# Six row scatters of a batch, one to each group of score units, with GpSimd in the order of the program text

## The chip, the cores and the metric

The kernel runs on one core of a Trainium2 chip. The metric is the device time of one execution in microseconds (us). A core has five engines that run their own instruction streams: TensorE (PE, matmuls and transposes; its weight loads are shown apart as PEld), VectorE (DVE), ScalarE (ACT), GpSimd (POOL) and SyncE (SP, which here only issues DMAs). They wait for each other through semaphores. An engine executes its own instructions in order, so an instruction that waits holds everything behind it on that engine. DMAs are issued by SyncE (loads of q, k, v, and transposes) and by GpSimd (weight loads that cast to bf16, and the indirect row scatters and gathers), and are carried by the same 16 DMA engines.

## The reference

Two stages. The first is attention with chunk selection: for 4 batches of 8 heads, 768 positions and 64 dimensions, keys are grouped into chunks of 32. Each query scores every chunk by an upper bound and keeps the best six; scores outside of them, or ahead of the query, are masked.

```python
ub = np.sum(np.maximum(q[..., None, :] * k_min, q[..., None, :] * k_max), axis=-1)
ub = np.where(causal, ub, -1e9)
top_chunks = np.argsort(ub, axis=-1)[..., -6:]
scores = np.where(sel & (pos[:, None] >= pos[None, :]), scale * q @ k.T, -1e9)
attn = softmax(scores);  attn_out = attn @ v
```

The second takes the 3072 tokens (512 values each: 8 heads of 64) through a layer of eight experts, one per token:

```python
logits = x @ w_gate
expert_idx = np.argmax(logits, axis=1)          # one expert per token
gate_w = softmax(logits)[expert_idx]
out[token] = gate_w * (np.maximum(x @ w1[e], 0) @ w2[e])
```

## The kernel before

**Units of work.** Two heads of a batch form a head pair; there are 16, numbered i = 0 to 15, four to a batch (b = i // 4, hp = i % 4). A pair's scores are cut into seven units: units 0 and 1 for the first half of the queries, 2 to 6 for the second half. `scores` (line 273) makes a unit's scores on PE, takes the exponential on ScalarE into a tile tagged Pa (units 0 and 2) or Pr (the others), and, where a block lies on the diagonal, lets GpSimd zero the future with `affine_select` (line 298). Units 0, 1, 5 and 6 have such blocks, 1 and 6 two each. `attend` (line 301) multiplies a unit by v on PE (line 311) and adds the unit into an accumulator on VectorE (line 323).

**The loop.** Lines 616 to 662 run over i, and for each i over four groups g = 0 to 3, with the units (0, 1), (2, 3), (4, 5) and (6) of `groups`. Into these groups the program text places, ahead of time or behind it, the steps of neighbouring pairs: the transposes and reductions of the next pairs' keys and queries (`prep`), the bound and selection of pair i + 1 (`ub` in g = 0, line 234; `select` in g = 1, lines 242 to 253; `mask` in g = 2, lines 260 to 263), the loads of q, k and v three pairs ahead (`load`), a quarter of an expert's weights per step (`load_w`, line 173), and the steps of the router for earlier pairs. `ud` (g = 1, lines 339 to 347) forms the denominators and the pair's part of the gate logits, `lgp` (g = 3) adds them to the batch's logits `lg` on GpSimd (lines 362 and 365), `x0` (g = 3) and `x1` (g = 0 of the pair after) transpose the attention output back to rows and write them, normalised, as bf16 into `xrow0` and `xrow1` (line 373).

**Routing of a batch.** When a batch's four pairs are done, `route_steps(b)` chooses the expert (`logits`, lines 381 to 408), ranks the tokens within their experts (`rank`, lines 410 to 431, which ends in the row numbers `sli` on VectorE), and `scatter` (lines 433 to 446) writes the 768 rows of 1032 bytes to a DRAM table `xs_dram`, sorted by expert: six indirect DMAs of 128 rows, numbered u = 0 to 5, even u from `xrow0` and odd u from `xrow1`. The three calls for batch b - 1 stand in the second pair of batch b: logits after g = 0, rank in g = 1, scatters after g = 2 and g = 3. So the pairs i = 5, 9 and 13 carry them. The last batch is routed after the loop.

**Buffers.** `xrow` has three buffers for two tiles per batch, so the `xrow1` of a batch lies where the `xrow0` of the batch before lay. Its first write is `x1` of the batch's first pair, in g = 0 of the batch's third pair (i = 6, 10, 14), and it has to wait until scatters 0, 2 and 4 of the batch before have read their rows. The small PSUM tiles (tag `m`) rotate through three buffers.

**The experts.** After the loop, and from g = 1 of the last pair on, tiles of 128 sorted rows are gathered (`gather`, line 533), transposed by a DMA on SyncE (`x_in`, line 545, with a copy `ti` of the token numbers on VectorE, lines 548 and 550), multiplied by w1 (`up`, line 562), transposed again (line 568), multiplied by w2 (`down`, line 578), scaled (line 582) and scattered to the output (line 583). Gathers 0 to 10 need only the rows of the first three batches, the others those of the last batch too.

**What sets the order.** A scheduler orders each engine's instructions by its own estimate of when they are ready. For engines named in `tc.manual_schedule` the order is that of the program text. Before, this is PE alone in the loop, PE and SyncE after it. A few instructions are pinned with `keep_in_program_order` (weight loads among them). GpSimd's other work, the selects, casts (line 219), additions to `lg`, scatters and gathers, is placed by the scheduler.

Of the kernel before, what the change touches and what calls it, by code (L numbers as in the profile page):

```python
# [15 lines left out]
AX = mybir.AxisListType  # L16
PE = mybir.EngineType.PE
SP = mybir.EngineType.SP


@with_exitstack
def kernel(
# [157 lines left out]
    def load(i):  # L180
        b, hp = divmod(i, HP)
        for nm, src in (("k", k), ("q", q), ("v", v)):
            t_ = ld.tile([128, NT, 2, D], FP32, tag=nm, bufs=2 if nm == "v" else 1)
            for hd in range(2):
                nc.sync.dma_start(out=t_[:, :, hd, :],
                                  in_=src[b, 2 * hp + hd].rearrange("(t p) d -> p t d", p=128))
            st[i][nm] = t_
# [407 lines left out]
    route = {b: route_steps(b) for b in range(B)}  # L595
# [5 lines left out]
    def run(d, j, *names):  # L601
        if j in d:
            for n in names:
                d[j][n]()

    with tc.manual_schedule(engines={PE}):
        load(0)
        load(1)
        load(2)
        run(prep, 0, "k0", "k1", "q0", "q0e", "q1", "q1e", "kse", "ub", "select")  # L610
        run(prep, 1, "k0")
        run(prep, 0, "mask")
        scores(0, 0)
        scores(0, 1)
        run(prep, 1, "k1", "q0", "q0e", "q1", "q1e", "kse")
        for i in range(NP):
            b, hp = divmod(i, HP)
            for g in range(4):
                if g == 0:
                    scores(i, 2)  # L620
                    scores(i, 3)
                    run(rout, i - 2, "x1")
                elif g == 1:
                    scores(i, 4)
                    scores(i, 5)
                    run(prep, i + 1, "select")
                    if hp == 1 and b > 0:
                        route[b - 1][1]()
                elif g == 2:
                    scores(i, 6)  # L630
                    run(prep, i + 2, "k0")
                    run(prep, i + 1, "mask")
                else:
                    run(rout, i - 1, "lgp", "x0")
                    if i + 1 < NP:
                        scores(i + 1, 0)
                        scores(i + 1, 1)
                    run(prep, i + 2, "k1", "q0", "q0e", "q1")
                    if i + 3 < NP:
                        load(i + 3)  # L640
                for u in groups[g]:
                    attend(i, u)
                if g == 3:
                    run(prep, i + 2, "q1e", "kse")
                if g == 0:
                    run(prep, i + 1, "ub")
                    if hp == 1 and b > 0:
                        route[b - 1][0]()
                if g == 1:
                    run(rout, i - 1, "ud")  # L650
                if hp == 1 and b > 0 and g == 2:
                    route[b - 1][2]((0, 2, 4))
                if hp == 1 and b > 0 and g == 3:
                    route[b - 1][2]((1, 3, 5))
                for n in range(NW):
                    if wq[n] == 4 * i + g:
                        load_w(n)
                if i == NP - 2 and g == 2:
                    table(True)
                if i == NP - 1 and g == 1:  # L660
                    for j in range(4):
                        gather(j)
                        x_in(j)
        rt = rout[NP - 1]
        r = route[B - 1]
        run(rout, NP - 2, "x1")
        with tc.manual_schedule(engines={SP}):
            up(0)
            rt["ud"]()
            gather(4)  # L670
            up(1)
            x_in(4)
            rt["lgp"]()
            rt["x0"]()
            rt["x1"]()
            r[0]()
            gather(5)
            up(2)
            x_in(5)
            down(0)  # L680
            r[1]()
            gather(6)
            r[2](range(6))
            table(False)

            def tiles(lo, hi):
                for j in range(lo, hi + 2):
                    if lo == 0 and j < 3:
                        continue
                    if lo == 0 and j + 4 < hi:  # L690
                        gather(j + 4)
                    if j < hi:
                        up(j)
                    if lo == 0 and j + 3 < hi:
                        x_in(j + 3)
                    if j - 2 >= lo:
                        down(j - 2)

            tiles(0, JM)
    rest = nc.values_load(more[0:1, 0:1], min_val=NA - JM, max_val=JT - JM,  # L700
                          skip_runtime_bounds_check_because="the table counts at most one part tile per expert")
    with tc.If(rest > 0):
        with tc.manual_schedule(engines={PE, SP}):
            for j in range(JM, JT):
# [41 lines left out]
```

## Time and profile before

| | us |
|---|---|
| median of 9 runs | 382.86 |
| lowest and highest | 381.7 and 386.67 |
| the profiled execution | 382.29 |
| its span in the profile | 380.4 |
| granted PE clock, mean | 0.962 |
| attention, twelve periods: from the bound of pair 3 to that of pair 15 (56.15 to 238.25) | 182.10 |
| from there to the first expert matmul (238.25 to 261.43) | 23.18 |
| from there to the last output scatter of the timeline (261.43 to 369.39) | 107.96 |

Lines of the profile name the engine, the source line (L436), the operation, the tile written and the tiles read, and the times. A row of a timeline begins with the start in us from the span's start and the busy time; in brackets stands the idle time of the engine before it and what ended it. A row of the table of stages gives, for a stretch of time, its length, the busy time and number of instructions of each engine, the granted PE clock as a share of full speed, the share of time that the DMA engines were busy (it can pass 1 a little in short stretches) and the GB/s they moved. In the experts' part one stretch stands out: from 278.0 to 287.6 PE is busy for 5.90 us of 9.60 at a clock of 0.77, and ScalarE waits 7.6 us for something that the profile names only as remote.

### The profile page before, as it was taken

The numbers are of one execution on the slowest core, as the hardware profiler recorded it, in microseconds if no ns is written. First come the engines' busy times: TensorE is split into PE (matmuls) and PEld (weight loads), VectorE is DVE, ScalarE is ACT, GpSimd is POOL, SyncE is SP. The second block draws the span as 40 slices with busy tenths as digits, with TensorE's granted clock in tenths as the row PEclk, the third lists the DMA queues.
The fourth block names the chain that finished last, engine by engine and source line by source line (L and its number), as shares of the span: only waits on it lengthen the run. The fifth ranks groups of instructions, "written<-read, shape, count | busy, mean of one in ns | idle before, by whom it ended". The sixth has DMA issues, their size and how long they took to land.

```text
span 380.4 us, 7332 instructions
## 1 busy us (share of the span) xinstructions
PE 339.7 (89%) x2214; PEld 171.2 (45%) x2224; DVE 229.1 (60%) x781; ACT 236.5 (62%) x397; POOL 182.2 (48%) x298
## 2 busy tenths in 40 slices
PE   2588999999979999998999997988969899999990
PEld 1244465455444554553545544433523344444430
DVE  7547898898997898995988997956710000000000
ACT  1477797797795977965779777552414454545440
POOL 9232442352386343467423438376375556565231
PEclk9859999999999999998999998999987999999997
DMA  9445989999979989869998985334958999998741
GB/s 171 80 93 101 179 155 155 190 167 155 179 163 208 178 160 181 163 138 203 161 188 165 168 153 93 88 72 112 146 146 179 206 233 190 210 219 182 189 122 47
DMA packets 138182, 59.81 MB, mean 157 GB/s; under 512 B 122779, under 2 KB 130973, under 8 KB 138144
## 3 DMA queue, kind: packets, MB, share of 16 engines
q1 hardware_dynamic: 120608, 29.91, 40.9%
q0 software_dynamic: 17536, 29.42, 40.0%
q8 instruction: 20, 0.33, 0.3%
q14 instruction: 18, 0.15, 0.2%
HBM read 56.14 MB, written 10.51 MB: 175 GB/s over the span
## 4 chain that ended last, share of the span: by engine, by line
PE 50%; ACT 12%; issue 12%; DVE 8%; POOL 7%; DMA 5%; another core or an unknown queue 3%; SPq 0%; POOLq 0%; ACTq 0%
PE po L311 13%; PE ps L289 7%; PE ph L562 6%; PE pu L234 5%; PE py L578 5%; PE pt L371 3%; ACT Pr L294 3%; PE pu L339 3%; ACT QSB L263 3%; ACT QSB L262 3%; PE pu L344 3%; POOL out_dram L583 2%; PE pt L242 2%; PE pt L210 2%
## 5 line engine op out<-in xcount | busy, mean ns | idle before, releaser
L323 DVE TENSOR_TENSOR Pa<-Pa,Pr 128x768 f32<-128x768 f32 (+2 forms) x112 | 82.2, 734 | 6.2 <-PE po L311 4.1
L298 POOL TENSOR_SCALAR_AFFINE_SELECT Pr<-Pr 128x256 f32<-128x256 f32 x80 | 33.7, 440 | 72.8 <-ACT Pr L294 71.9
L294 ACT ACTIVATE Pr<-ps 128x768 f32<-128x768 f32 (+2 forms) x112 | 65.3, 628 | 3.5 <-PE ps L289 3.1
L578 PE MATMUL py<-w_all,hT 128*128 x219 | 54.1, 385 | 4.2 <-issue 2.7
L289 PE MATMUL ps<-QSB,KTE 128*128 128x384 bf16 (+2 forms) x288 | 50.0, 297 | 3.6 <-ACT QSB L263 2.5
L583 POOL DMA_INDIRECT out_dram<-y,ti x28 | 27.8, 994 | 42.3 <-ACT y L582 29.9
L289 PEld LDWEIGHTS <-KTE 128*128 128x128 bf16 x288 | 24.5, 99 | 35.0 <-issue 26.7
L578 PEld LDWEIGHTS <-hT 128*128 128x128 bf16 x224 | 22.0, 98 | 32.6 <-issue 5.4
L436 POOL DMA_INDIRECT xs_dram<-xrow,sli x24 | 26.9, 1121 | 13.8 <-issue 5.3
L562 PE MATMUL ph<-w_all,KTE 128*128 x117 | 29.2, 391 | 0.3 <-issue 0.2
L347 ACT ACTIVATE ud<-pu 128x384 f32<-128x384 f32 x16 | 7.9, 492 | 34.2 <-PE pu L344 34.2
L294 ACT ACTIVATE Pa<-ps 128x768 f32<-128x768 f32 x32 | 26.0, 812 | 3.7 <-PE ps L289 3.0
L562 PE MATMUL ph<-w_all,QSB 128*128 x102 | 24.9, 379 | 2.0 <-issue 1.8
L173 POOL DMA_DIRECT2D w_all<-in_moe_w_dram x32 | 24.5, 765 | 0.0
L202 DVE TENSOR_REDUCE kmx<-pt 128x12 f32<-128x384 f32 x32 | 17.7, 554 | 7.8 <-PE pt L200 7.7
L219 POOL CAST QSB<-qT 64x384 bf16<-64x384 f32 x32 | 16.2, 515 | 11.6 <-DVE qT L217 11.2
L582 ACT ACTIVATE y<-py,xg 128x512 f32<-128x512 f32 x16 | 11.0, 688 | 14.4 <-PE py L578 6.3
L245 DVE TENSOR_TENSOR ubm<-pt,cbias 128x144 f32<-128x144 f32 x32 | 8.6, 302 | 18.8 <-PE pt L242 18.6
L373 DVE TENSOR_TENSOR xrow<-pt,rec 128x384 bf16<-128x384 f32 x32 | 17.6, 551 | 2.9 <-DMA xs_dram<-xrow,sli 2.2
L533 POOL DMA_INDIRECT xg<-xs_dram,grow x16 | 17.0, 1061 | 4.8 <-issue 4.4
L550 DVE TENSOR_TENSOR ti<-xg,inv_i 128x1 int32<-128x1 int32 x9 | 1.4, 159 | 29.6 <-DMA xg<-xs_dram,grow 28.4
L562 PEld LDWEIGHTS <-KTE 128*128 128x128 bf16 x120 | 12.0, 100 | 15.8 <-issue 3.3
(294 smaller groups left out, 659.1 us busy)
## 6 DMA issues: line engine op xcount, KB each, us to landing
w_all<-in_moe_w_dram POOLq DMA_DIRECT2D x32, 512.0 KB
out_dram<-y,ti POOLq DMA_INDIRECT x28
t__188<-in_k_dram SPq DMA_DIRECT2D x2, 192.0 KB
t__191<-in_q_dram SPq DMA_DIRECT2D x2, 192.0 KB
t__194<-in_v_dram SPq DMA_DIRECT2D x2, 192.0 KB
t__203<-in_v_dram SPq DMA_DIRECT2D x2, 192.0 KB
t__197<-in_k_dram SPq DMA_DIRECT2D x2, 192.0 KB
t__200<-in_q_dram SPq DMA_DIRECT2D x2, 192.0 KB
```

What stands on the lines that cost most here:

```text
L173: d = nc.gpsimd.dma_start(out=dst, in_=src.rearrange("(c p) f -> p c f", p=128))
L202: nc.vector.tensor_reduce(s["kmx"][:, ts(hf, 12)], pk, AX.X, ALU.max)
L234: nc.tensor.matmul(pu[64 * hf:64 * hf + 64, :], lhsT=w_[:], rhs=s[f"{nm}{hf}"][:], start=(nm == "qT"), stop=(nm == "qA"), skip_group_check ...
L289: nc.tensor.matmul(pv[:, hd, :], lhsT=kte[:, hd, ts(kb, 128)], rhs=qsb[:, hd, ds(qb * 384 + 384 - w, w)], start=True, stop=True, skip_grou ...
L294: nc.scalar.activation(P[:, :, ds(c0, w)], pv, AF.Exp)
L298: nc.gpsimd.affine_select(out=pd, in_=pd, pattern=[[0, 2], [1, 128]], compare_op=ALU.is_ge, fill=0.0, base=0, channel_multiplier=-1)
L311: nc.tensor.matmul(po[64 * hd:64 * hd + 64, 384 - w:384], lhsT=vt[:, kb, hd, :], rhs=P[:, hd, ds(c0, w)], start=first, stop=last and n == ...
L323: nc.vector.tensor_tensor(acc[:, :, 384 - w:384], acc[:, :, 384 - w:384], P[:, :, ds(c0, w)], ALU.add)
L436: d = nc.gpsimd.indirect_dma_start(out=xs_dram[:], out_offset=bass.IndirectOffsetOnAxis(ap=sli[:, u:u + 1], axis=0), in_=bst[b][f"xrow{u % ...
L562: nc.tensor.matmul(ph[:, fh, :], lhsT=xT[:, c, :], rhs=w_all[:, ds(wo + (c * F + fh * 512), 512)], start=(c == 0), stop=(c == NDC - 1), sk ...
L578: nc.tensor.matmul(py[:], lhsT=hT[:, c, :], rhs=w_all[:, ds(wo + (W1W + c * DM), DM)], start=(c == 0), stop=(c == NFC - 1))
L583: d = nc.gpsimd.indirect_dma_start(out=out[:], out_offset=bass.IndirectOffsetOnAxis(ap=fs[j]["ti"], axis=0), in_=y[:], in_offset=None, bou ...
```

## The change

The scatters of a batch are called one at a time, after six groups in a row, from g = 2 of the second pair to g = 3 of the third, in the order u = 0, 2, 4, 1, 3, 5. GpSimd joins PE in the list of engines whose instructions keep the order of the program text within the loop (and, since the block after the loop is nested in it, there too). What is scattered and the number of DMAs stay. Line numbers in the changed kernel are one higher from line 19 to the loop.

```diff
+POOL = mybir.EngineType.Pool
...
-    with tc.manual_schedule(engines={PE}):
+    with tc.manual_schedule(engines={PE, POOL}):
...
-                if hp == 1 and b > 0 and g == 2:
-                    route[b - 1][2]((0, 2, 4))
-                if hp == 1 and b > 0 and g == 3:
-                    route[b - 1][2]((1, 3, 5))
+                slot = 4 * hp + g - 6
+                if b > 0 and 0 <= slot < 6:
+                    route[b - 1][2]((2 * (slot % 3) + slot // 3,))
```

In the order of the built program, the changed kernel has on GpSimd, in a pair that routes: the two selects of unit 6, scatter 0, a weight load, the addition to `lg`, the selects of units 0 and 1 of the next pair, two casts, and then, already for the next pair, scatters 2 and 4 and a weight load, the select of unit 5, scatter 1, the selects of unit 6, scatter 3, a weight load, and behind that pair's casts scatter 5. In the last pair: scatter 5, the select of unit 5, gathers 0 to 3, the selects of unit 6, two additions to `lg`, gather 4, two additions, gather 5, the first output scatter, gather 6, the last batch's six scatters, gather 7. On VectorE line 373 of the third pair moves from ahead of the accumulations to between the two additions of line 245.

## The prediction

> **What bounds the kernel now.** I read the page's first part, then cut the span into the periods of a head pair with the table of stages, because the chain that ended last repeats itself nearly word for word from 56 to 238 us. A period runs from one start of the bound matmul (line 234) to the next.
>
> ```profile
> PE 339.7 (89%) x2214; PEld 171.2 (45%) x2224; DVE 229.1 (60%) x781; ACT 236.5 (62%) x397; POOL 182.2 (48%) x298
> ```
> ```profile
> 84.53:98.73 14.20, 14.12 (x111) 7.57 (x108) 12.53 (x40) 11.64 (x22) 5.32 (x13) 1.00 0.94 171
> 98.73:115.80 17.07, 14.86 (x123) 7.93 (x120) 15.47 (x56) 13.28 (x25) 10.34 (x15) 1.00 0.89 160
> 115.80:129.93 14.13, 14.05 (x110) 7.49 (x108) 12.07 (x39) 10.33 (x19) 8.61 (x17) 1.00 1.08 202
> ...
> 158.30:176.62 18.32, 16.12 (x123) 8.55 (x120) 15.69 (x56) 13.28 (x25) 11.27 (x15) 0.93 0.83 154
> 176.62:191.46 14.84, 14.51 (x111) 7.61 (x110) 12.33 (x38) 10.33 (x19) 7.49 (x16) 0.98 1.07 195
> ...
> 219.88:238.25 18.37, 16.13 (x122) 8.59 (x120) 15.67 (x56) 13.24 (x25) 10.65 (x15) 0.92 0.67 117
> ```
> Columns: stretch, length, then busy time of PE, PEld, DVE, ACT, POOL, clock, DMA share, GB/s. A plain period is 14.2 us and PE is busy for 14.1 of it: PE is the bound, with nothing to gain. The three periods that route a batch (head pairs 5, 9, 13) take 17.07, 18.32 and 18.37 us. Why, the timeline of GpSimd, then of PE and VectorE, shows (first routing period, then the same wait of PE and of VectorE in the others):
>
> ```profile
> 105.64 1.58 POOL L436 DMA_INDIRECT xs_dram<-xrow,sli  x1 [2.29 <-DVE sli L429]
> 107.21 1.46 POOL L298 TENSOR_SCALAR_AFFINE_SELECT Pr<-Pr 128x256 f32<-128x256 f32 x2
> 108.84 1.29 POOL L436 DMA_INDIRECT xs_dram<-xrow,sli  x1 [0.17 <-issue]
> 110.44 0.98 POOL L436 DMA_INDIRECT xs_dram<-xrow,sli  x1 [0.30 <-issue]
> 111.40 0.80 POOL L173 DMA_DIRECT2D w_all<-in_moe_w_dram  x1
> 112.50 1.04 POOL L436 DMA_INDIRECT xs_dram<-xrow,sli  x1 [0.30 <-issue]
> 113.53 0.34 POOL L362 TENSOR_TENSOR lg<-lgt 128x48 f32<-128x48 f32 x1
> 113.77 0.46 POOL L298 TENSOR_SCALAR_AFFINE_SELECT Pa<-Pa 128x256 f32<-128x256 f32 x1
> ```
> ```profile
> 114.28 0.87 PE L311 MATMUL po<-Pa,t__1094 128*64 128x384 f32 x4 [1.82 <-POOL Pa L298]
> ...
> 173.85 1.50 PE L311 MATMUL po<-Pa,t__1951 128*64 128x384 f32 x4 [1.82 <-POOL Pa L298]
> ...
> 235.42 1.55 PE L311 MATMUL po<-Pa,t__2808 128*64 128x384 f32 x4 [1.83 <-POOL Pa L298]
> ```
> ```profile
> 114.10 0.56 DVE L373 TENSOR_TENSOR xrow<-pt,rec 128x384 bf16<-128x384 f32 x1 [0.56 <-DMA xs_dram<-xrow,sli]
> ...
> 174.51 0.56 DVE L373 TENSOR_TENSOR xrow<-pt,rec 128x384 bf16<-128x384 f32 x1 [1.37 <-DMA xs_dram<-xrow,sli]
> ...
> 234.98 0.56 DVE L373 TENSOR_TENSOR xrow<-pt,rec 128x384 bf16<-128x384 f32 x1 [0.28 <-DMA xs_dram<-xrow,sli]
> ```
> The diagonal select of Pa had its input at about 109.5 (ACT 108.68 + 0.81) and ran at 113.77, behind three scatters and a weight load; PE stood 1.82 us for it, three times. The last rows are the price list for what the change touches: line 373 writes the buffer that the scatters 0, 2, 4 read, and goes on only when scatter 4 has landed: 3.66, 4.50 and 3.41 us after that scatter's start (110.44, 170.01, 231.57).
>
> **The change part by part.** Times within a period are counted from U, the start of line 234 (in a plain period 84.53).
>
> *1. No scatter between the selects of a routing period.* The built program's order on GpSimd is now: two selects of unit 6, scatter 0, weight load, lg, Pa, Pr, two casts, scatters 2 and 4. Scatter 0 (1.29) from 106.8, weight load (0.80), lg (0.34): Pa could go at 109.5 and be done at 109.9, while PE asks for it at 112.46 (111.91 + 0.55). Cover 2.5 us, so the three waits go: 1.82 + 1.82 + 1.83 = -5.5.
>
> *2. The slow clock behind them.* After the second and third wait the next matmuls took 1.50 instead of 0.87 and the clock of the period is 0.93 and 0.92; after the first, the same wait cost nothing. By periods: (18.32 + 14.84) - (17.07 + 14.13) = 2.0 for the second; 18.37 - 17.07 = 1.3, and about 0.3 after it, for the third. Gone: -3.5 (ends 0 and -3.6).
>
> *3. Scatter 0 no longer waits for sli in front of the selects.* The selects of unit 6 ran at 107.21, ready at 106.0; VectorE waited 0.15 for them and PE 0.23 at line 210. Some 0.3 each: -0.9 (ends 0 and -1.2). What stays is routing itself: VectorE has 15.47 busy us in such a period against 12.53, so I expect some 15.0 us, not 14.2.
>
> *4. The new wait.* Scatter 4 is now the last but in the next period: behind the second cast (end U - 0.7) and scatter 2 it starts near U + 0.8. Line 373 of the first head pair of the new batch has to wait for it and stands in VectorE's new order between the two additions of line 245. Behind it wait the second addition, the maxima and nsel (line 253), and for nsel PE's mask transposes (line 260), then ACT's copies and the next scores. From plain rows: nsel ends 3.03 us after line 373 starts (0.48, then 87.31 to 89.86), and PE asks at U + 6.09 (90.62). So line 373 may start at U + 3.06 for free. With a landing of 3.66 it starts at U + 4.46: PE stands 1.40. I take 3.66 (the middle row) for the first two batches and 3.41 for the third, where no loads of q, k, v follow: 1.40 + 1.40 + 1.15 = +3.9. The ends: the fastest gather's 2.83 us (249.31 to 252.14) gives 0.57 each, +1.7; 4.50 everywhere gives 2.24 each, +6.7. The transposed tile that line 373 reads is held as long; the next user is line 200 at U + 5.66, not late at 3.66.
>
> [...]
>
> *5. Clock behind the new wait.* Waits of 1.82 cost 0.1, 2.0 and 1.6 in clock; the gaps of 0.52, 0.44 and 1.10 in head pair 15 cost none (0.99 over 238.25 to 261.43). The new ones lie between: I take the mean of the three, once, +1.2 (ends 0 and 3 x 1.8 = 5.4).
>
> [...]
>
> *6. Head pair 15 and the gathers.* Scatter 5 of the third batch now stands before that pair's last selects, and gather 0 waits for it (issued about 250.3, landed by 253.7 at 3.41), then the gathers 0 to 3 (four of 1.31 with their gaps, 5.2 us) come between the select of unit 5 (253.8) and those of unit 6. PE's gaps of 0.52 (POOL) and 0.44 (VectorE, held by ti of line 548) go, the one of 1.10 at unit 6 becomes about 2. Net +0.2 (ends -1.0 and +1.5).
>
> *7. Tail.* Gathers 4 to 7 leave 256.6 to 263 and go behind lg, the first output scatter and the six last scatters: about 262.5, 268.5, 273.3, 282.4. SyncE takes their transposes in its fixed order at 268.99, 272.10, 275.57 and 285.44, so 4 and 5 are in time, 6 about 0.6 late, 7 level; behind a late one waits only the next hT. ScalarE's 7.6 us wait at 275.5 and PE's slow stretch from 278 to 287.6 cover these; if they went, gather 7 would become the next thing late. Later gathers come one tile (3.45) later with some 10 us of lead: 0. The six last scatters start 1.3 later; nothing reads them before gather 11 at 291. Weight loads only move by a few us, needed from 261: 0. DMA counts are the same.
>
> Sum: -5.5 - 3.5 - 0.9 + 3.9 + 1.2 + 0.2 = -4.6. The profiled run took 382.29 (span 380.4 and 1.9 around it), 0.57 under the median of 382.86. 382.29 - 4.6 = 377.7.
>
> **The rivals.**
> - *The wait is hidden* (scatter 4 lands within 2.8 us): for it, the gathers' 2.83 us and that the burst of SP loads ends near U + 1.6; against it, the three scatter rows. -9.9 + 0.2 + 0 to 1.7 = 372.6 to 374.3.
> - *The clock falls at every new wait*: for it, two of three before; against it, the new waits are shorter. -9.9 + 3.9 + 0.2 + 5.4 = -0.4: 381.9, no change.
> - *Slower*: the same place, line 373, with landings of 4.5 and more in each batch, since scatter 4 now follows a weight load and shares the engines with the next loads, and the clock falls as well: 6.7 + 5.4 + 0.2 - 9.9 = +2.4, 384.7. It decides from 3.3 us lost per batch (9.9 / 3); against it, only one row of three was 4.50.
> - *The change does nothing*, because another wait ends last in PE's place: against it, PE is named behind POOL in all three, and in the first VectorE ended KD at 113.53, which line 234 would ask for at 112.46 + 1.44 = 113.90 at the earliest. If VectorE held PE nearly as long, only what part 2 saves without the new wait's cost remains: 380 to 382.
>
> **How the numbers follow.** My forecast 0.54, hidden wait 0.15, clock at every wait 0.12, nothing 0.06, slower 0.13. About 0.5% (1.9 us) is what a measurement of this kernel can tell from no change. Faster by more (under 380.9): forecast, hidden, and a third of nothing: 0.71. Within: clock, rest of nothing: 0.16. Slower: 0.13. The likeliest case's own range is 375 to 380.5; for 8 in 10 the range leaves out half of the hidden wait's times and the slower case: 373.2 to 383.0.
>
> **What would show it.** Right: PE's three waits on Pa gone, routing periods near 15.0; line 373 waiting 1 to 2 us on the scatter in the periods after, PE waiting for nsel there, those periods near 15.6. Wrong: those periods at 14.2 (wait hidden) or above 17 (clock below 0.95); a gap of more than 3 us at unit 6 in pair 15; a longer or shorter stretch at 278 to 288, which nothing in this profile explains and which I hold fixed.

## The result, and the profile after

The changed kernel takes 392.74 us (median of 10 runs, 391.1 to 396.0); the kernel before took 383.78 us on the same chips (31 runs, 379.5 to 389.5). The ratio is 1.027, with a 95% interval from 1.023 to 1.030: slower by 2.7%, where the prediction had 377.7 us and a range up to 383.0. The profiled execution took 391.39 us, with a span of 389.6; that of before took 382.29, with a span of 380.4. Line numbers of the changed kernel are one higher than before: the 373 of the prediction is 374 here.

The first part of the page of the changed kernel shows an unchanged amount of work; PE's share fell by a point:

```profile
PE 342.4 (88%) x2214; PEld 172.3 (44%) x2224; DVE 227.8 (58%) x781; ACT 236.3 (61%) x397; POOL 180.3 (46%) x298
```

The table of stages of the changed kernel, cut at the starts U of line 235 (its first matmul in the timeline, 0.17 us before the point that the prediction counts from; columns as in the prediction: length, then busy time of PE, PEld, DVE, ACT, POOL, clock, DMA share, GB/s):

```profile
85.17:99.36 14.19, 14.11 (x113) 7.56 (x110) 12.52 (x39) 11.64 (x22) 5.30 (x13) 1.00 0.92 169
99.36:114.14 14.78, 14.63 (x124) 7.93 (x122) 14.49 (x55) 11.78 (x23) 6.81 (x14) 1.00 0.93 142
114.14:133.82 19.68, 15.78 (x112) 8.47 (x110) 12.54 (x39) 11.63 (x22) 10.21 (x17) 0.91 0.95 182
...
162.19:176.98 14.79, 14.64 (x125) 7.94 (x122) 14.50 (x55) 11.79 (x23) 6.83 (x14) 1.00 0.86 140
176.98:196.54 19.56, 15.55 (x113) 8.32 (x111) 12.68 (x40) 11.64 (x22) 10.27 (x17) 0.91 1.00 189
224.90:239.72 14.82, 14.66 (x125) 7.93 (x122) 14.53 (x56) 11.79 (x23) 6.20 (x13) 1.00 0.75 116
239.72:267.60 27.88, 22.03 (x158) 10.61 (x154) 18.54 (x59) 12.16 (x21) 15.54 (x20) 0.94 0.29 72
267.60:380.23 112.63, 105.05 (x475) 45.87 (x484) 13.60 (x77) 47.71 (x57) 58.71 (x61) 0.95 0.83 180
```

The last two stages of the kernel before, cut the same way (head pair 15, then the expert stretch):

```profile
238.03:261.43 23.40, 21.05 (x157) 9.84 (x154) 18.01 (x61) 10.66 (x18) 14.38 (x21) 0.98 0.39 91
261.43:371.10 109.67, 103.35 (x475) 45.76 (x484) 12.90 (x75) 47.54 (x57) 56.10 (x59) 0.97 0.83 180
```

The three routing periods are what the change was to repair, and it did: 14.78, 14.79 and 14.82 us, where before they were 17.07, 18.28 and 18.36 between the same starts. The period behind each lost it again: 19.68 and 19.56 (before 14.12 and 14.88), and pair 15, which follows the third, 27.88 (23.40). In the first of them PE stands for 19.68 - 15.78 = 3.9 us, and its busy time is 1.67 longer than a plain period's 14.11 at a clock of 0.91. The balance over the span: start 0.8, routing periods -9.3, the two periods behind them +10.2, pair 15 +4.5, experts +3.0: 9.2, the difference of the spans.

The timeline of the changed kernel shows the place; GpSimd first, then the three waits of VectorE, then PE behind the first of them:

```profile
107.84 1.10 POOL L437 DMA_INDIRECT xs_dram<-xrow,sli  x1 [0.17 <-issue]
108.92 0.77 POOL L174 DMA_DIRECT2D w_all<-in_moe_w_dram  x1
...
113.97 1.52 POOL L437 DMA_INDIRECT xs_dram<-xrow,sli  x1 [0.27 <-issue]
...
115.80 1.03 POOL L437 DMA_INDIRECT xs_dram<-xrow,sli  x1 [0.30 <-issue]
...
121.50 0.56 DVE L374 TENSOR_TENSOR xrow<-pt,rec 128x384 bf16<-128x384 f32 x1 [4.33 <-DMA xs_dram<-xrow,sli]
...
184.26 0.56 DVE L374 TENSOR_TENSOR xrow<-pt,rec 128x384 bf16<-128x384 f32 x1 [4.26 <-DMA xs_dram<-xrow,sli]
...
244.95 0.56 DVE L374 TENSOR_TENSOR xrow<-pt,rec 128x384 bf16<-128x384 f32 x1 [2.14 <-DMA xs_dram<-xrow,sli]
```
```profile
122.11 0.55 PE L201 MATMUL pt<-ident_f,t__1532 128*128 128x128 f32 x3 [1.98 <-DVE xrow L374]
124.57 0.47 PE L261 MATMUL pt<-ident_b,nsel 128*64 128x128 bf16 x5 [1.92 <-DVE nsel L254]
...
124.93 2.52 PE L312 MATMUL po<-Pr,t__1094 128*64 128x384 f32 x7
```

The rows at 107.84, 113.97 and 115.80 are the scatters 0, 2 and 4; between 0 and 2 stands a weight load of 512 KB. Scatter 4 starts at U + 1.66 and line 374 goes on at 121.50, which is 5.70 us later (5.63 in the second batch, from 178.63; 3.58 in the third, from 241.37). Behind line 374 PE stands twice, for the PSUM tile that line 374 reads (line 201 wants its slot) and for nsel; then seven matmuls take 2.52 us, at a clock of 0.55 from 124.9 to 127.5. No wait of PE on Pa is left.

In pair 15 of the changed kernel PE stands for nsel, behind the third of these waits, and for unit 6's selects, which came behind the gathers 0 to 3:

```profile
248.29 0.74 PE L261 MATMUL pt<-ident_b,nsel 128*64 128x128 bf16 x5 [2.58 <-DVE nsel L254]
...
266.10 0.87 PE L312 MATMUL po<-Pr,t__3008 128*64 128x256 f32 x8 [2.54 <-POOL Pr L299]
```

### The profile page after: what moved, and what is told of

The parts are those of the page before. It is cut to its first block, busy times and chain, and to the rows that moved or that the text cites. A ratio compares the mean times of both kernels' runs of the same rounds, so it can differ in the third digit from the quotient of the medians.

```text
span 389.6 us, 7326 instructions
## 1 busy us (share of the span) xinstructions
PE 342.4 (88%) x2214; PEld 172.3 (44%) x2224; DVE 227.8 (58%) x781; ACT 236.3 (61%) x397; POOL 180.3 (46%) x298
## 4 chain that ended last, share of the span: by engine, by line
PE 35%; issue 19%; POOL 12%; DVE 12%; ACT 11%; DMA 8%; POOLq 1%; SPq 0%; ACTq 0%; DVEq 0%
PE po L312 10%; PE ps L290 5%; POOL xg L534 4%; DMA xs_dram<-xrow,sli 4%; POOL out_dram L584 4%; DMA t__692<-in_q_dram 3%; PE pu L235 3%; ACT Pr L295 3%; PE ph L563 3%; PE pt L372 3%; ACT QSB L264 2%; DVE Pa L324 2%; ACT QSB L263 2%; PE pu L340 2%; PE pu L345 2%
## 5 line engine op out<-in xcount | busy, mean ns | idle before, releaser
L324 DVE TENSOR_TENSOR Pa<-Pa,Pr 128x768 f32<-128x768 f32 (+2 forms) x112 | 80.9, 723 | 4.0 <-PE po L312 2.1
L299 POOL TENSOR_SCALAR_AFFINE_SELECT Pr<-Pr 128x256 f32<-128x256 f32 x80 | 32.8, 428 | 74.8 <-ACT Pr L295 73.5
L563 PE MATMUL ph<-w_all,KTE 128*128 x117 | 31.0, 396 | 4.1 <-issue 2.7
L437 POOL DMA_INDIRECT xs_dram<-xrow,sli x24 | 25.9, 1079 | 6.4 <-issue 6.0
L374 DVE TENSOR_TENSOR xrow<-pt,rec 128x384 bf16<-128x384 f32 x32 | 17.6, 551 | 11.1 <-DMA xs_dram<-xrow,sli 10.7
L220 POOL CAST QSB<-qT 64x384 bf16<-64x384 f32 x32 | 16.0, 500 | 15.7 <-DVE qT L218 13.8
L366 POOL TENSOR_TENSOR lg<-lg,lgt 128x48 f32<-128x48 f32 x24 | 6.8, 284 | 34.0 <-DVE lgt L357 29.2
L263 ACT ACTIVATE QSB<-pt 24x768 bf16<-24x768 bf16 x16 | 12.8, 797 | 15.6 <-PE pt L261 15.3
L246 DVE TENSOR_TENSOR ubm<-pt,cbias 128x144 f32<-128x144 f32 x32 | 8.8, 302 | 19.5 <-PE pt L243 16.3
```

What stands on the lines that cost most here:

```text
L263: nc.scalar.activation(qsb[64:64 + NCH, 0, :], pt[0:NCH, :], AF.Copy)
L299: nc.gpsimd.affine_select(out=pd, in_=pd, pattern=[[0, 2], [1, 128]], compare_op=ALU.is_ge, fill=0.0, base=0, channel_multiplier=-1)
L324: nc.vector.tensor_tensor(acc[:, :, 384 - w:384], acc[:, :, 384 - w:384], P[:, :, ds(c0, w)], ALU.add)
L437: d = nc.gpsimd.indirect_dma_start(out=xs_dram[:], out_offset=bass.IndirectOffsetOnAxis(ap=sli[:, u:u + 1], axis=0), in_=bst[b][f"xrow{u % ...
L563: nc.tensor.matmul(ph[:, fh, :], lhsT=xT[:, c, :], rhs=w_all[:, ds(wo + (c * F + fh * 512), 512)], start=(c == 0), stop=(c == NDC - 1), sk ...
```

## The experiments

All ratios are to runs of the kernel before on the same chip; its median was 383.8 us beside the changed kernel, 382.8 beside the last two runs below, and 377.4 to 379.2 on the chips of the others. "Routing" are the three routing periods, "behind" the periods after the first two, "pair 15" the time from its U to the first expert matmul, "experts" from there to PE's last instruction, all in us from the one profiled execution. "Landing" is the time from the start of scatter 4 to the start of line 374, for the three batches; it is given where line 374 waited for the scatter. The kernel without loads leaves 2.4 MB of loads out and ran once (381.6 us), so it has no ratio. On the chips of those others the kernel before was not profiled, so where a ratio and the periods of the table don't agree, the place of the difference can't be read.

| kernel | ratio (95%) | routing | behind | pair 15 | experts | landing |
|---|---|---|---|---|---|---|
| before | 1 | 17.1 / 18.3 / 18.4 | 14.1 / 14.9 | 23.4 | 109.7 | 3.66 / 4.50 / 3.41 |
| changed | 1.027 (1.023 to 1.030) | 14.8 / 14.8 / 14.8 | 19.7 / 19.6 | 27.9 | 112.6 | 5.70 / 5.63 / 3.58 |
| split alone | 1.021 (1.014 to 1.028) | 16.4 / 16.4 / 16.9 | 18.9 / 18.8 | 26.5 | 104.1 | 7.14 / 7.75 / 7.25 |
| order alone | 1.002 (0.998 to 1.006) | 15.5 / 15.4 / 15.5 | 14.2 / 14.4 | 24.4 | 111.3 | 4.67 / - / - |
| scatters 2, 4 earlier | 1.058 (1.051 to 1.065) | 14.8 / 14.8 / 14.8 | 21.5 / 20.6 | 30.7 | 110.2 | 7.95 / 6.58 / 7.07 |
| no q, k, v loads | - | 14.8 / 14.8 / 14.8 | 16.4 / 16.3 | 27.4 | 110.4 | 3.71 / 3.34 / 4.22 |
| weight load after | 1.011 (1.001 to 1.021) | 14.8 / 14.8 / 14.8 | 17.9 / 16.1 | 25.3 | 111.2 | 3.95 / 3.22 / 2.85 |
| both of these moves | 1.032 (1.020 to 1.044) | 14.8 / 14.8 / 14.8 | 20.1 / 18.6 | 27.6 | 109.7 | 5.27 / 4.45 / 4.42 |
| four buffers | 1.008 (1.003 to 1.012) | 14.9 / 14.9 / 14.9 | 15.4 / 15.3 | 23.8 | 109.4 | no wait |
| order alone, scatters spread | 0.991 (0.987 to 0.996) | 15.5 / 15.4 / 15.5 | 14.1 / 14.8 | 24.3 | 113.4 | 4.54 / 5.05 / - |

**The two halves of the change, each alone.** GpSimd's order left to the planner, with the scatters split:

```diff
-    with tc.manual_schedule(engines={PE, POOL}):
+    with tc.manual_schedule(engines={PE}):
```


> Only the split of the scatters; GpSimd's order is again the planner's. The planner puts scatter 0 in front of the selects of unit 6, and 2 and 4 with a weight load in front of Pa's select: nearly the old order. Theory A (the late scatter 4 costs, and it is late only because GpSimd keeps program order): no wait of line 374 over 1.5 us, PE waits on Pa again, less than 1.82 us since two scatters and not three are in front of it; 380 to 384 us, the kernel before within 0.5%. Rival B (the split itself makes scatter 4 late): line 374 waits over 3 us and the time is above 389.

and GpSimd in program order, with the scatters in two groups of three:

```diff
-                slot = 4 * hp + g - 6
-                if b > 0 and 0 <= slot < 6:
-                    route[b - 1][2]((2 * (slot % 3) + slot // 3,))
+                if hp == 1 and b > 0 and g == 2:
+                    route[b - 1][2]((0, 2, 4))
+                if hp == 1 and b > 0 and g == 3:
+                    route[b - 1][2]((1, 3, 5))
```


> Only GpSimd in program order; the scatters are issued in two groups of three as before (0, 2, 4 behind unit 6's selects, 1, 3, 5 behind the casts). Unit 6's selects are no longer behind a scatter, so 0, 2, 4 run from about 107.5 to 111.2 and Pa's select comes at about 112, PE asks for it at 112.5. Theory A: PE's wait on Pa is 0 to 0.5 us, scatter 4 starts near 110 and line 374 waits under 1.5 us: the routing gain of some 8 us less the 4 to 5 us that head pair 15 and the tail lose, 378 to 382 us. Rival B (the order alone makes the loss): above 389. Rival C (three scatters in front of Pa hold PE as before): waits of 1.8 us on Pa, 386 to 389.

The split alone is slower by 2.1%, with an interval that takes in the whole loss of 2.7%; the order alone makes no difference that can be measured, though its routing periods are 1.6 to 2.9 us shorter. Timeline of the split alone (GpSimd, PE, VectorE, then PE again), first batch:

```profile
105.94 1.59 POOL L437 DMA_INDIRECT xs_dram<-xrow,sli  x1 [2.29 <-DVE sli L430]
...
108.93 0.74 POOL L174 DMA_DIRECT2D w_all<-in_moe_w_dram  x1
...
111.34 1.03 POOL L437 DMA_INDIRECT xs_dram<-xrow,sli  x1 [0.30 <-issue]
...
113.92 0.87 PE L312 MATMUL po<-Pa,t__1094 128*64 128x384 f32 x4 [1.16 <-POOL Pa L299]
...
118.48 0.56 DVE L374 TENSOR_TENSOR xrow<-pt,rec 128x384 bf16<-128x384 f32 x1 [3.87 <-DMA xs_dram<-xrow,sli]
...
130.16 0.85 PE L211 MATMUL pt<-ident_f,t__1535 128*128 128x128 f32 x6 [2.41 <-DMA t__1535<-in_q_dram]
```

Timeline of the order alone, the same stretch, and PE in the expert stretch:

```profile
110.49 0.98 POOL L437 DMA_INDIRECT xs_dram<-xrow,sli  x1 [0.30 <-issue]
...
111.47 0.79 POOL L174 DMA_DIRECT2D w_all<-in_moe_w_dram  x1
...
113.12 0.87 PE L312 MATMUL po<-Pa,t__1094 128*64 128x384 f32 x4 [0.59 <-POOL Pa L299]
...
115.16 0.56 DVE L374 TENSOR_TENSOR xrow<-pt,rec 128x384 bf16<-128x384 f32 x1 [0.43 <-DMA xs_dram<-xrow,sli]
...
285.82 3.57 PE L563 MATMUL ph<-w_all,KTE 128*128 x8 [4.96 <-DMA KTE<-QSB]
```

What the rows at 111.34 and 110.49 have in common is scatter 4 at nearly the same time as in the kernel before (110.44). What differs is the weight load. In one group of three, the three scatters follow each other on the queue and the weight load of that step comes behind them; split, the weight load stands between 0 and 2. Scatter 4 then lands after 7.14 us and not after 3.66 to 4.67. So of the two theories on the split run the rival held: splitting makes the scatter that is waited for late, whoever orders GpSimd. It is not the only late transfer there: behind line 374 PE stands 1.71 and 2.33 us in the two periods (line 243), and then 2.41 and 1.69 us more at line 211 for the load of the next q, which in the first landed 14.0 us after its issue. The order alone repairs the waits on Pa to 0.49 to 0.59 us and leaves line 374 with 0.43. Its pair 15 is 1.0 us longer than before and its expert stretch 1.6; the rest of where its gain went is not shown, since the kernel before was not profiled on that chip.

**What makes the landing late.** First the loads of q, k and v for head pairs 8 and 12 taken away:

```diff
-                    if i + 3 < NP:
+                    if i + 3 in (8, 12):
+                        st[i + 3].update({nm: st[i + 2][nm] for nm in ("k", "q", "v")})
+                    elif i + 3 < NP:
                         load(i + 3)
```


> The changed kernel without the loads of q, k and v for head pairs 8 and 12: those that SyncE starts around 110 to 117 and 173 to 180 us, while scatter 4 of batches 0 and 1 is on its way. (Pairs 8 and 12 compute on the values of pairs 7 and 11, so this kernel leaves 2.4 MB of loads out.) The weight load that GpSimd issues 6.9 us ahead of scatter 4 stays. Theory F (scatter 4 waits its turn behind that weight load on the software queue; the loads of SyncE only slow the weight load down): the landing takes 3.4 to 3.7 us as in the third batch, line 374 waits about 2.1, the periods 114-134 and 177-197 become 16.5 to 17.5. Theory S (the loads of SyncE alone share the engines with the scatter): the same landing of 3.4 to 3.7. Rival R (neither: the landing of the split scatter is long by itself): 5.6 us as before. This run decides only on R; the next one on F against S.

Then these loads kept, and the weight load moved behind scatter 4:

```diff
+    for n, g4 in ((13, 24), (22, 40), (31, 56)):
+        wq[n] = g4
```


> The changed kernel with one weight load per batch moved: the one that GpSimd issues right behind scatter 0 (6.9 us ahead of scatter 4) now goes behind scatter 4. SyncE's loads stay. Theory F (order on the software queue): scatter 4 of batches 0 and 1 lands in 3.4 to 4.5 us and no longer in 5.7, line 374 waits 2 to 3 us where it waited 4.3, the two periods drop from 19.7 and 19.6 to 16.5 to 18. Theory S (sharing with SyncE's loads): 5.5 to 5.8 us, the periods unchanged.

VectorE's waits without the loads:

```profile
119.11 0.56 DVE L374 TENSOR_TENSOR xrow<-pt,rec 128x384 bf16<-128x384 f32 x1 [2.35 <-DMA xs_dram<-xrow,sli]
...
178.26 0.56 DVE L374 TENSOR_TENSOR xrow<-pt,rec 128x384 bf16<-128x384 f32 x1 [1.96 <-DMA xs_dram<-xrow,sli]
```

and with the loads, but the weight load behind the scatter, VectorE's timeline and the table of the two periods:

```profile
119.54 0.56 DVE L374 TENSOR_TENSOR xrow<-pt,rec 128x384 bf16<-128x384 f32 x1 [2.59 <-DMA xs_dram<-xrow,sli]
...
179.80 0.56 DVE L374 TENSOR_TENSOR xrow<-pt,rec 128x384 bf16<-128x384 f32 x1 [1.84 <-DMA xs_dram<-xrow,sli]
```
```profile
113.93:131.78 17.85, 15.66 (x113) 8.33 (x110) 12.45 (x39) 11.64 (x22) 11.37 (x18) 0.90 1.03 184
174.94:191.08 16.14, 14.35 (x113) 7.52 (x111) 12.70 (x40) 11.64 (x22) 12.99 (x18) 1.00 0.99 159
```

Without the loads the scatter, which started at 115.40 and 174.92, lands in 3.71 and 3.34 us; with the weight load moved, from 115.59 and 176.58, in 3.95 and 3.22. Taking away either brings the old landing back, so sharing with SyncE's loads alone (theory S) is not the cause here: the landings of the two runs differ by 0.24 and 0.12 us. What would fit both runs is that a weight load 6.9 us ahead is done by then when nothing else runs, and with 1.15 MB of q, k and v in the same stretch is not, so that the scatter waits behind it; that is my reading and was not shown, since the end of the weight load itself was not read from a trace. Where the weight load is nearer (2.4 us ahead in the split alone), the landing is 7.25 us in the third batch too, in which SyncE only loads one v. The whole time, too, followed: 1.011 with the one load moved, where the changed kernel had 1.027. The landing is not all of the loss, though: with the old landing back the four periods are still 2.0 to 3.7 us above a plain one of 14.19, because scatter 4 starts at U + 1.6 to 1.7 and PE still stands 1.62 to 1.95 us for nsel; in one of the four the clock is 0.90 as well.

**Scatters 2 and 4 earlier.** Since the scatter was late, I moved it up, in front of the two casts:

```diff
                         scores(i + 1, 1)
+                    if hp == 1 and b > 0:
+                        route[b - 1][2]((2, 4))
                     run(prep, i + 2, "k1", "q0", "q0e", "q1")
...
-                slot = 4 * hp + g - 6
-                if b > 0 and 0 <= slot < 6:
-                    route[b - 1][2]((2 * (slot % 3) + slot // 3,))
+                if hp == 1 and b > 0 and g == 2:
+                    route[b - 1][2]((0,))
+                slot = 4 * hp + g - 8
+                if b > 0 and 0 <= slot < 3:
+                    route[b - 1][2]((1 + 2 * slot,))
```


> The changed kernel, with scatters 2 and 4 of a batch moved up: behind the diagonal selects of the next pair (Pa, Pr) and in front of the two casts, instead of behind the casts; 1, 3 and 5 stay one per group. Scatter 4 then starts some 4 us before the period's end instead of 1.5 us after it. Theory A (the new wait of line 374 for the landing of scatter 4 and what follows it in the clock are most of the loss): the periods 114-134 and 177-197 (19.7 and 19.6 us) go back to 14.3 to 14.8, the third one loses its 2.1 us of wait; 5 + 5 + 2.5 = 12 to 13 us less than the changed kernel, 378 to 382 us. Rival B (the loss is the clock, which falls wherever PE is pressed in these periods, or the casts, now 2 us later, hold PE in place of line 374): 388 us and more, and a PE wait at the scores of the pair after. Rival C (the loss is in head pair 15 and the tail): under 3 us less than the changed kernel.

and then with the weight load moved as well, to groups 23, 39 and 55:

> The first experiment (scatters 2 and 4 in front of the casts) with the weight load that stood between scatter 0 and scatter 2 moved behind the casts. In the first experiment scatter 4 took 7.9 us to land, 4.3 us behind that weight load. Theory F: it lands within 3.4 to 4.6 us, near 117 us or 3.4 us after the period's start; line 374 is free until 3.06, so it waits under 1 us and PE under 0.5; all periods 14.1 to 14.9, U of pair 15 near 230; 8 to 10 us less than the kernel before in the loop, less some 4 us in pair 15 and the tail: ratio 0.98 to 0.995. Theory S: scatter 4 still takes 6 us and more since SyncE's loads run in the same stretch; periods of 17 and more, ratio above 1.01.

The first is slower than the kernel that it was to mend; the second is no faster (1.032, 1.020 to 1.044, where the changed kernel had 1.027). Timelines, of the first and then of the second:

```profile
108.38 0.76 POOL L174 DMA_DIRECT2D w_all<-in_moe_w_dram  x1
...
112.67 1.03 POOL L437 DMA_INDIRECT xs_dram<-xrow,sli  x1 [0.30 <-DVE qT L218]
...
120.62 0.56 DVE L374 TENSOR_TENSOR xrow<-pt,rec 128x384 bf16<-128x384 f32 x1 [7.63 <-DMA xs_dram<-xrow,sli]
121.32 0.87 PE L243 MATMUL pt<-ident_f,ubT 128*128 128x128 f32 x3 [5.49 <-DVE xrow L374]
```
```profile
112.73 0.98 POOL L437 DMA_INDIRECT xs_dram<-xrow,sli  x1 [0.30 <-DVE qT L218]
...
118.00 0.56 DVE L374 TENSOR_TENSOR xrow<-pt,rec 128x384 bf16<-128x384 f32 x1 [4.91 <-DMA xs_dram<-xrow,sli]
118.70 0.88 PE L243 MATMUL pt<-ident_f,ubT 128*128 128x128 f32 x3 [2.77 <-DVE xrow L374]
```

The 7.95 us in the first go with the weight load 4.3 us ahead, as above. The second has none ahead and lands in 5.27, 4.45 and 4.42, while the same scatter 3 us later took 3.95, 3.22 and 2.85; SyncE's loads stand nearer ahead of it here (v 1.5 us ahead in the third batch, 4.1 there), so sharing with them may have its price too (the landings of the two kernels differ by 1.2 to 1.6 us), which no run tried by itself. And it loses more than that. Line 374 begins to wait at 118.00 - 4.91 = 113.09, or U - 0.6; in the changed kernel it begins at 121.50 - 4.33 = 117.17, or U + 3.0. VectorE's order is the planner's: with the scatter earlier, line 374 stands earlier too, in front of the additions of line 324. What I gave the transfer (some 3 us) the planner took away from it (3.6 us), and PE now stands at line 243, sooner than at line 261. None of the theories on record had this; theory F's landing of 3.4 to 4.6 us came in two batches of three, and it had the place of the wait wrong.

**The wait taken away.** Four buffers for xrow, paid for with three for Pr:

```diff
-            P = work.tile([128, 2, 384], FP32, tag="Pr", bufs=4, name="Pr")
+            P = work.tile([128, 2, 384], FP32, tag="Pr", bufs=3, name="Pr")
...
-                    bst[b][f"xrow{hf}"] = work.tile([128, 3, XW], BF16, tag="xrow", name="xrow", bufs=3)
+                    bst[b][f"xrow{hf}"] = work.tile([128, 3, XW], BF16, tag="xrow", name="xrow", bufs=4)
...
-        h_ = work.tile([128, F], BF16, tag="Pr", bufs=4)
+        h_ = work.tile([128, F], BF16, tag="Pr", bufs=3)
```


> The changed kernel with four buffers for xrow in place of three, paid for with three in place of four for Pr. Line 374 now writes a buffer whose last scatters are a batch older: the wait is gone without touching scatters, weights or loads. If the new wait and its clock are the loss in the loop: the periods 114-134 and 177-197 go to 14.2 to 14.9, the third batch loses 2.1 us of wait, 12 to 13 us less than the changed kernel (ratio to the kernel before 0.99 to 1.0). If the clock falls in these periods for another reason, the periods stay above 17. The price that three buffers for Pr could have shows as ScalarE's exponentials waiting for line 312 or 324.

Line 374 no longer waits for a scatter, and the two periods are, by the table of stages:

```profile
113.95:129.30 15.35, 14.10 (x112) 7.62 (x110) 12.61 (x39) 12.51 (x23) 12.38 (x17) 1.00 1.10 200
...
173.18:188.47 15.29, 14.11 (x112) 7.61 (x110) 12.58 (x39) 12.51 (x23) 12.24 (x17) 1.00 1.05 193
```

PE's busy time is a plain period's, and the clock, 0.91 in the changed kernel, is 1.00 with the wait gone. Against the changed kernel the two periods are 4.3 and 4.3 shorter and pair 15 is 4.1 shorter, 12.7 in the profile, as expected. Some 1.1 us per period stay, and PE stands them at line 211, for the transposes of the next q; the same line a period later:

```profile
125.29 0.85 PE L211 MATMUL pt<-ident_f,t__1535 128*128 128x128 f32 x6 [1.17 <-DVE kmn L204]
...
140.14 0.85 PE L211 MATMUL pt<-ident_f,t__1746 128*128 128x128 f32 x6 [0.72 <-DMA t__1746<-in_q_dram]
```

The second row names the load of q. The first names VectorE, but by the trace of that tile its load landed 7.5 to 7.8 us after its issue (from 116.73), so just before PE went on: with the scatters split, SyncE's load is late as well, as it was in the split alone. In time the four buffers give 1.008, not 0.99 to 1.0: 1.9% less than the changed kernel, about 7 us. The profiled execution was the fastest of its ten (376.27, median 380.97), so its 12.7 us are not those of the median, and where the others lose more is not shown.

**The expert stretch.** GpSimd in program order only up to pair 14:

```diff
+    inner = ExitStack()
-    with tc.manual_schedule(engines={PE, POOL}):
+    with tc.manual_schedule(engines={PE}), inner:
+        inner.enter_context(tc.manual_schedule(engines={POOL}))
...
+            if i == NP - 1:
+                inner.close()
```


> The changed kernel, but GpSimd keeps program order only up to head pair 14; in pair 15 and the expert tiles its order is the planner's again (gathers 0 to 3 partly behind unit 6's selects, gathers 4 to 7 early). Everything up to 238 us is the changed kernel's. Theory A: pair 15 loses 1.5 to 2 us less (the 2.5 us wait of PE for Pr becomes about 1.1) and the tail is the old 110.7 us instead of 113.7: 3 to 5 us less than the changed kernel, 388 to 390 us. Rival B (the tail's 3 us is chance, the clock or the stretch at 289-301, not the late gathers): within 1.5 us of the changed kernel.

The ratio is 1.029 (1.022 to 1.036), no better than the changed kernel: theory A falls. In the profile two things pull against each other. In the planner's order PE stood 5.5 us in pair 15 for selects, which came behind gathers, and pair 15 took 30.7 us (27.9 in the changed kernel); the expert stretch was 105.1 us (112.6), without the slow piece that the profiles of before and after both have. The profiled execution took 392.47 us where the median is 388.64, and 4.6 us of it lie before the first bound (at 16.08, not 11.48), so the two cannot be summed to the median. With program order, in every profile in which that slow piece is missing, PE stands 4.3 to 5.2 us in one place instead, as in the order alone at 285.82, and in the kernel with four buffers:

```profile
285.07 3.57 PE L563 MATMUL ph<-w_all,KTE 128*128 x8 [5.24 <-DMA KTE<-QSB]
```

(In the kernel with both moves the matmul's row, 4.30 us, names only "issue", but PE's weight load for it waited for the same tile:)

```profile
296.30 0.11 PEld L563 LDWEIGHTS <-KTE 128*128 128x128 bf16 x1 [3.56 <-DMA KTE<-QSB]
```

That is the tile of gather 7, which in program order is issued behind the six last scatters (277.27 in this kernel, 15 us later than before). So it was moved in front of them, in three kernels:

```diff
             gather(6)
+            gather(7)
             r[2](range(6))
...
-                    if lo == 0 and j + 4 < hi:
+                    if lo == 0 and 7 < j + 4 < hi:
```


> GpSimd in program order, the scatters in two groups of three as before (the third experiment), and gather 7 issued right behind gather 6, in front of the six last scatters, instead of behind them. In the third experiment the loop was 7.4 us shorter than the kernel before's, and then PE stood 5.0 us for the transposed rows of gather 7, issued 23 us into the expert stretch. Theory T (that order in the expert stretch is what ate the loop's gain): the 5.0 us wait goes, and the slow clock behind it: 5 to 8 us less than the third experiment, ratio 0.98 to 0.99 to the kernel before. Rival (another transfer is late next, or the stretch loses as much whatever the gathers do): ratio 0.995 to 1.005.

> The changed kernel with four buffers for xrow (three for Pr) and gather 7 in front of the six last scatters: both suspected losses of the change taken away. The run with the four buffers alone had 5.2 us of PE wait for gather 7 and a ratio of 1.0075. Theory T: 5 to 8 us less, ratio 0.986 to 0.995. Rival: 1.0 and above.

> The changed kernel with only gather 7 moved in front of the six last scatters; everything up to the expert stretch is unchanged, the new wait of line 374 too. Theory T: where PE and ScalarE aren't held by late instructions, 5 us and the clock behind them come back: ratio 1.005 to 1.015 where the changed kernel had 1.027. Rival (in the changed kernel PE's slow stretch from 289 to 301 covers gather 7, as the prediction had it): ratio 1.02 to 1.03.

Measured: 0.998 (0.995 to 1.001), 0.9985 (0.995 to 1.002) and 1.024 (1.018 to 1.030), some 0.3 to 0.9% less than without, clear of the intervals only with the four buffers, and not the 5 to 8 us of theory T. PE's row in the first of them says why:

```profile
289.62 3.33 PE L563 MATMUL ph<-w_all,KTE 128*128 x8 [3.89 <-DMA KTE<-xg]
```

The wait moved on to gather 8, the next one behind the scatters. So the scatters were spread, two behind each of the gathers 7, 8 and 9, in the kernel with the order alone; and the kernel before was profiled once more, unchanged:

```diff
             gather(6)
-            r[2](range(6))
...
                         gather(j + 4)
+                        if j < 6:
+                            r[2]((2 * j - 6, 2 * j - 5))
```


> GpSimd in program order with the scatters in two groups of three (the third experiment), and the six last scatters spread over the first expert tiles: two behind each of the gathers 7, 8 and 9, instead of all six in front of gather 7. Moving gather 7 alone in front of them passed PE's wait (5.0 us) on to gather 8 (3.9 us). Theory Q (the six scatters, 7.8 us in one piece on the queue, hold whatever gather is behind them): no PE wait on a gathered tile over 1.5 us, the expert stretch falls from 109-111 to 103-105 us, ratio to the kernel before 0.98 to 0.99. Rival (something else, the late instructions for instance, takes the same time there): 108 us and more, ratio 0.995 to 1.005.

> The kernel before, unchanged, profiled a second time. If the slow stretch 20 us into the expert tiles (instructions late on PE and ScalarE, clock 0.64 for 10 us) belongs to the kernel, it is there again and the expert stretch is 109 to 110 us; if it was that execution's, the stretch is 103 to 106 us, perhaps with a wait for gather 8 of about 2 us. The loop's periods, 17.1, 18.3 and 18.4 us for the three that route, should repeat within 0.2 us, with the slow clock perhaps in another of them.

PE's waits, summed over the whole span (us in total, times, longest), in the kernel with the scatters spread and then in the kernel before, profiled again; lines 562, 563 and 578 are the expert stretch, line 311 is the loop:

```profile
PE ph L563 <- issue: 4.7, 7, 1.0
```
```profile
PE po L311 <- POOL Pa L298: 5.5, 3, 1.8
...
PE py L578 <- issue: 2.2, 3, 1.0
PE ph L562 <- issue: 2.0, 3, 1.5
```

Spread, no gathered tile is waited for any more. The kernel is faster than the kernel before, 0.991 (0.987 to 0.996), and is the only one of this study that is. Against the kernel before on this same chip the three routing periods are 5.7 us shorter in the profile. The expert stretch is not short, though, but 113.4 us (108.8): in place of the 5 us the slow piece is there, PE standing 4.7 us in seven places for nothing that the profile shows, and the clock at 0.50 for 5 us. Theory Q was right on the wait and wrong on the stretch. The second profile of before repeats the first: routing periods 17.1, 17.4 and 17.6 with 15.7 behind the second (the slow clock lay elsewhere; 17.41 + 15.72 is 33.13 and 18.28 + 14.88 is 33.16), PE's three waits on Pa, and the slow piece with an expert stretch of 108.8 us. So that piece came in both profiled executions of the kernel before.

## Why the prediction was wrong

- **Parts 1 to 3, the gain (-9.9): right.** The three waits on Pa are gone, the routing periods are 14.8 us (15.0 foreseen), -9.3 by the periods; the slow clock that reached into the period of 14.88 (0.75 from 176.45 to 178.30) went as well (1.00 from 176.98 to 179.00), but is covered there by the new loss.
- **Part 4, the new wait (+3.9): the step that failed.** The place was right: line 373, between the two additions of line 245, nsel and PE's mask transposes behind it. The size was not. "With a landing of 3.66 it starts at U + 4.46" has two terms, and both were too small: scatter 4 starts at U + 1.66 (1.49 from the prediction's zero) and not U + 0.8, since the scatter before it took 1.52 us, with 0.27 and 0.30 of idle time around it, and it lands in 5.70, 5.63 and 3.58. My price rows came from scatters whose nearest weight load on the queue was 7.8 us or more ahead. The new order, which I had written out, puts one 6.9 us ahead, with the loads of q, k and v in between, and moving it away restores the old landing (3.95, 3.22, 2.85). With U + 7.36 for line 373, line 200 at U + 5.66 is late too, which I had excluded "at 3.66". (The third batch is not free of loads, as I had it: SyncE loads a v there, at 232.42 before and at 237.28 after.) PE stands 3.9 and 4.0 us in the two periods where I had 1.40.
- **Part 5, the clock (+1.2): mis-sized.** PE's busy time is 1.67 and 1.44 us above a plain period's; in pair 15 the clock is 0.57 from 247.7 to 251.7. It fell at all three (0.91 over each of the two periods), where I took one. The drop at each new wait, which I had only as a rival at 0.12, is what came here. It did not come at every wait: single waits of 1.92 and 1.75 us without the loads left the two periods' clock at 1.00. Parts 4 and 5 together, against plain periods of 14.19: 5.5 + 5.4, and in pair 15 some 3.6 (4.5 less part 6): +14.5 instead of +5.1.
- **Part 6, pair 15 (+0.2):** the gap at unit 6 is 2.54 (about 2 foreseen), of the two gaps that were to go one stayed (0.48, at line 312); some +0.9, within the ends.
- **Part 7, the tail (0):** the cover held in the changed kernel's profile, whose slow piece lies from 289 to 301, and gather 7's tile is late inside it. The stretch is 3.0 us longer, which I had not. In kernels without that piece the loss I had named for that case came, 4.3 to 5.2 us at gather 7. Of the 13.7 us between the forecast and the profiled execution, parts 4 and 5 make some 9.4, this stretch 3.0, a later start 0.8 and part 6 0.7.
- **The rivals.** The slower one, 384.7 us, had the mechanism: this line, scatter 4 behind a weight load and among the next loads, the clock as well, from 3.3 us per batch on. I gave it 0.13, "only one row of three was 4.50", though none of the three rows had a weight load near ahead of it. Its price was too low by 8 us: it took 4.5 as the worst landing, and nothing for the expert stretch. Hidden wait and no effect are excluded by the waits; that the clock falls at every new wait is true of the changed kernel and is part of the loss.

What stays open: what PE stands for some 20 us into the expert stretch (last section), a piece with which that stretch took 113.4 us (scatters spread) where the wait for a gather made it 111.3 (order alone), and why q's load is so late when the scatters are split.

## What to carry to other kernels

The same transfer took 2.85 us in one place on the queue and 7.95 in another, so its time from issue to landing is not its own: before you move it, or split a group of transfers, write down what stands ahead of it on the same queue, and take the price from a row with the same thing ahead. If an instruction is placed by a planner, it can move along with the transfer that it waits for, so that issuing the transfer earlier can lengthen the wait (here from 2.59 to 4.91 us, the weight load moved in both); take the wait away with another buffer, or keep the group together. And a small transfer that is late at the head of a queue can pass its wait on to the next one when it alone is moved, as the 4.96 us of gather 7 became 3.89 of gather 8 here: look at what stands ahead of both on the queue.

## What I had not expected of the hardware

- The same scatter of 132 KB took between 2.85 and 7.95 us from start to landing. With 512 KB of weights 2.4 to 4.3 us ahead on the queue it took 6.58 to 7.95 us; with them 6.9 us ahead it took 5.70 and 5.63 while SyncE loaded q, k and v (3.95 and 3.22 with the weights behind it), and without these loads 3.71 and 3.34.
- The piece of the expert stretch in which PE stands for nothing that the profile shows (in the changed kernel PE is busy for 7.61 us of the 12.00 from 289 to 301, at a clock of 0.64) is there in four profiles of three kernels (twice in the kernel before, the changed kernel, the one with the scatters spread), and in each of them no matmul of PE is shown waiting there for a gathered tile. In the other eleven PE stands for one, between 2.0 and 5.2 us, and no such piece is seen. In the kernel with the scatters spread, taking the one away brought the other; why was not tried.
